# A kernel of linear attention and two feed-forward blocks: its unit loop written as one order, y in its own PSUM banks, a new order for the first units, and the decode steps of the last stage moved

## The chip, the cores and the metric

The kernel runs on one core of one Trainium2 chip. The metric is device time in microseconds, from the start to the end of one execution. Inputs and output lie in the chip's memory (HBM). The reference computes in float32, and the kernel keeps that precision on TensorE by splitting numbers into a high and a low part (below).

## The reference

Attention runs for 4 batches, 8 heads, 768 steps and a head width of 48; its output is a matrix `x` of 3072 tokens by 384. Two feed-forward blocks follow.

```python
for t in range(S):                                  # attention, per batch and head
    cur = einsum('bhd,bhe->bhde', u[None] * k_t, v_t)
    y_t = einsum('bhd,bhde->bhe', r_t, state + cur)
    state = w_t[..., None] * state + einsum('bhd,bhe->bhde', k_t, v_t)

h = x @ w_in                                        # first block, 384 -> 1024
e = exp(h - max(h)); solu = h * e / (sum(e) + 1e-9)
ln = (solu - mean(solu)) / sqrt(var(solu) + 1e-6) * g_ln
x = ln @ w_out                                      # 1024 -> 384

h = x @ w_in2                                       # second block, 384 -> 2048
out = maximum(0.01 * h, h) @ w_out2                 # 2048 -> 384
```

## The kernel before

**Numbers.** The weights of the feed-forward blocks arrive as float64 words. The kernel decodes them itself: one step on VectorE takes the exponent (L112), ScalarE turns it into a float's exponent (L114), and four more VectorE instructions (L120 to L126) make the value. Each float32 operand of a large product is then split into a rounded high part (a ScalarE copy, names in `h`) and the rest (a subtraction, names in `l`), and each product is three products: high by high, high by low, low by high (`passes`).

**Units.** The 3072 tokens are 24 units of 128; unit i is chunk i // 4 of batch i % 4. One unit goes through these steps, each a Python function that issues a few instructions:

- `load_tr`, `load_nat`: loads from SyncE's (SP's) queue. `prep1` to `prep4`, `prep_k`: two scans along time and products with r and k on VectorE (`prep_k` on GpSimd from unit 5 on). `prep_check`: a test of w on ScalarE. `prep_state`, `prep_bonus`, `prep_vd`: GpSimd; `prep_diag`: VectorE.
- `att_scores`: four transposes of k (L441, into the PSUM bank PK) and 32 products of k and r (L445, into PA). `att_evac_s` and `att_evac_k` take them out of PSUM. `att_u`: 32 products that give the state's increments (L465, also PA). `att_mid`, `att_mul_next`, `att_state`: the state, on VectorE (ScalarE for units 0 to 3), GpSimd, VectorE.
- `att_y`: 64 small products that add up y (L499, L509, L518) in PA. `att_x`: two VectorE additions that read y. `x_t`: three transposes into PZ[0] (L530); `x_hi`, `x_lo`: the split of x.
- `mm1`: h in two halves of nine products (L547, into PH). `soft_max` (maximum on VectorE, exponential on ScalarE), `soft_z` (product on VectorE, a factor on GpSimd), `soft_c`, `soft_q` (ScalarE). `z_t`: eight transposes into both PZ banks (L573), `z_hi`, `z_lo`: their split in two halves each.
- `mm2`: after units 4, 5, ... one product of the block's second matrix for a group of three units, in two halves of twelve products (L596, PO or PK); `mm2_out` sends it to HBM.

**Order.** Everything stands in a `manual_schedule`: each engine works off its instructions in the order in which the program names them, and waits for what the others owe it. The functions are called in three ways. The first units (0 to 12, with the parts of others that belong there) follow a list, the text `FIRST` (L31), in which the decode of the first block's weights, `w1_a` to `w1_d`, is mixed with the units. Then a loop (L847 to L906) does units 12 to 22, and a written tail (L916 to L979) the rest. In the loop, the small products of a unit stand in three places: scores, then half an `mm2`, `att_u`, `z_t` and `mm1`, then y, then the other half of `mm2`.

**Last stage.** The second feed-forward block has 96 steps (6 groups of 512 tokens by 16 chunks of the 2048 columns). Step n does `mm3`: nine products into one of two PSUM buffers `h2` (L753), then a scaled copy on ScalarE (L760), a maximum on VectorE that also reads the buffer (L761) and a rounding copy on ScalarE (L762). `gw_sub` is the low part, on VectorE (L767), which reads L762's result. `mm4` for step n - 2 (L777) is nine products that read both parts. The weights of this block are decoded in `dec_step`, one of 32 chunks a time in three phases (so 34 calls): L112 and L114 of a new chunk, L731 (ScalarE) for an older one, L120 to L126 of the one before, and L732 (VectorE). Two calls stand at the end of the loop, five in the tail, and one in each step of the last stage until the chunks are done, except in steps 3, 7 and 11:

```python
g, c = order[n]
mm3(g, c)
if n % 4 != 3 or n > 12:
    dec_step()
gw_sub(g, c)
...
if 2 <= n < len(order) - 1:
    mm4(*order[n - 2])
```

At the start, all four parts of the first block's weights are issued among the first units' loads (`load_w1i`, `load_w1o`, L796 to L803), the first of them from ScalarE's queue.

Of the kernel before, what the change touches and what calls it, by code (L numbers as in the profile page):

```python
# [31 lines left out]
load_nat 2; att_scores 0; w1_a; prep_state 1; w1_a; w1_a; att_evac_s 0; att_evac_k 0; att_u 0; att_mid 0;
prep1 1; w1_c; w1_d; w1_b; w1_b; w1_b; w1_b; att_mul_next 0; prep_check 1; prep_diag 0; prep_k 1; prep_vd 0;
prep_check 2; prep2 1; att_state 0; w1_c; w1_d; w1_c; w1_a; prep3 1; prep4 1; load_tr 3; w1_d; att_y 0;
w1_c; w1_b; w1_d; att_x 0; w1_c; w1_d; load_nat 3; att_scores 1; x_t 0; w1_c; x_hi 0; prep1 2; w1_a; w1_a;
att_evac_s 1; prep2 2; prep_bonus 1; att_evac_k 1; att_u 1; x_lo 0; mm1 0 0; w1_b; w1_d; w1_c; prep3 2;
att_mid 1; w1_a; att_mul_next 1; mm1 0 1; prep_diag 1; w1_b; att_state 1; prep_vd 1; prep_check 3; att_y 1;
w1_a; w1_d; w1_a; w1_b; w1_b; w1_c; w1_d; w1_c; att_x 1; prep_bonus 2; soft_max 0; w1_d; x_t 1; x_hi 1;
prep_k 2; prep4 2; load_tr 4; load_nat 4; att_scores 2; att_evac_k 2; prep_diag 2; prep_vd 2; soft_z 0;
soft_c 0; att_evac_s 2; att_u 2; w1_c; prep1 3; x_lo 1; z_t 0; soft_q 0; prep_k 3; z_hi 0 0; mm1 1 0; prep2  # L40
3; prep3 3; mm1 1 1; att_mid 2; w1_a; z_hi 0 1; w1_a; w1_a; w1_b; att_mul_next 2; w1_d; w1_c; w1_d; z_lo 0
0; w1_b; w1_c; att_state 2; att_y 2; soft_max 1; prep_check 4; w1_b; prep4 3; load_tr 5; w1_b; prep_bonus 3;
w1_d; w1_c; att_x 2; x_t 2; x_hi 2; w1_d; soft_z 1; soft_c 1; x_lo 2; prep_diag 3; prep1 4; load_nat 5;
att_scores 3; prep_vd 3; att_evac_s 3; prep_state 2; mm1 2 0; att_evac_k 3; w1_c; att_u 3; mm1 2 1; att_mid
3; prep2 4; z_lo 0 1; z_t 1; prep_check 5; prep3 4; prep4 4; w1_d; prep_k 4; load_tr 6; att_mul_next 3; z_hi
1 0; att_state 3; att_y 3; prep1 5; soft_q 1; soft_max 2; z_lo 1 0; prep_bonus 4; att_x 3; load_nat 6;
att_scores 4; att_evac_k 4; prep_state 3; soft_z 2; att_evac_s 4; x_t 3; x_hi 3; prep_state 4; x_lo 3; att_u
4; prep_bonus 5; prep_check 6; z_hi 1 1; att_mid 4; att_mul_next 4; prep_diag 4; prep_vd 4; prep2 5; prep3
5; prep_diag 5; mm1 3 0; mm1 3 1; prep_k 5; att_state 4; z_lo 1 1; att_y 4; soft_c 2; soft_q 2; soft_max 3;
prep4 5; load_tr 7; z_t 2; z_hi 2 0; att_x 4; load_nat 7; att_scores 5; z_lo 2 0; x_t 4; prep_bonus 6;  # L50
soft_z 3; att_evac_k 5; x_hi 4; x_lo 4; prep_vd 5; mm2 0 0 0; att_evac_s 5; prep1 6; prep_k 6; mm1 4 0; z_hi
2 1; z_lo 2 1; prep_state 5; att_u 5; att_mid 5; prep2 6; att_mul_next 5; att_state 5; soft_c 3; mm1 4 1;
prep1 7; soft_q 3; z_t 3; soft_max 4; att_y 5; mm2 0 0 1; prep3 6; prep4 6; load_tr 8; att_x 5; load_nat 8;
att_scores 6; z_hi 3 0; prep_diag 6; z_lo 3 0; x_t 5; z_hi 3 1; z_lo 3 1; prep_state 6; prep_vd 6; prep_k 7;
soft_z 4; mm2_out 0 0; mm2 0 1 0; x_hi 5; x_lo 5; mm1 5 0; att_evac_k 6; att_evac_s 6; att_u 6; mm1 5 1;
prep2 7; prep3 7; soft_c 4; soft_q 4; att_mid 6; prep4 7; att_mul_next 6; att_state 6; prep_check 7; load_tr
9; prep_state 7; z_t 4; z_hi 4 0; z_hi 4 1; att_y 6; soft_max 5; z_lo 4 0; prep1 8; mm2 0 1 1; mm2_out 0 1;
att_x 6; load_nat 9; att_scores 7; prep_bonus 7; att_evac_k 7; soft_z 5; x_t 6; x_hi 6; z_lo 4 1; mm2 0 2 0;
soft_c 5; att_evac_s 7; att_u 7; x_lo 6; prep_diag 7; mm1 6 0; prep_vd 7; att_mid 7; att_mul_next 7;
prep_check 8; z_t 5; prep2 8; prep3 8; z_hi 5 0; soft_q 5; z_hi 5 1; prep_k 8; att_state 7; att_y 7; prep4  # L60
8; load_tr 10; att_x 7; z_lo 5 0; mm1 6 1; soft_max 6; prep_bonus 8; prep_bonus 9; load_nat 10; att_scores
8; att_evac_s 8; mm2 0 2 1; z_lo 5 1; prep_state 8; att_evac_k 8; soft_z 6; x_t 7; att_u 8; mm2_out 0 2; mm2
1 0 0; att_mid 8; x_hi 7; x_lo 7; mm1 7 0; prep_check 9; att_mul_next 8; mm1 7 1; soft_c 6; z_t 6; soft_q 6;
prep1 9; prep_diag 8; prep2 9; z_hi 6 0; z_hi 6 1; prep3 9; att_state 8; prep4 9; soft_max 7; z_lo 6 0; z_lo
6 1; prep_state 9; prep_vd 8; att_y 8; prep_k 9; load_tr 11; mm2 1 0 1; mm2_out 1 0; att_x 8; x_t 8; x_hi 8;
load_nat 11; att_scores 9; prep1 10; soft_z 7; prep_diag 9; mm2 1 1 0; att_evac_k 9; prep_bonus 10;
att_evac_s 9; att_u 9; x_lo 8; prep2 10; prep3 10; prep_check 10; mm1 8 0; prep4 10; prep_vd 9; soft_c 7;
z_t 7; att_mid 9; z_hi 7 0; mm1 8 1; prep_diag 10; att_mul_next 9; att_state 9; att_y 9; z_lo 7 0;
prep_check 11; prep1 11; soft_q 7; soft_max 8; mm2 1 1 1; z_hi 7 1; prep_k 10; load_tr 12; prep_k 11;
prep_bonus 11; att_x 9; prep2 11; prep_state 10; soft_z 8; mm2_out 1 1; x_t 9; x_hi 9; load_nat 12;  # L70
att_scores 10; att_evac_k 10; x_lo 9; att_evac_s 10; mm2 1 2 0; att_u 10; soft_c 8; att_mid 10; soft_q 8;
att_mul_next 10; z_lo 7 1; prep_vd 10; mm1 9 0; mm1 9 1; z_t 8; att_state 10; att_y 10; prep3 11; prep4 11;
load_tr 13; mm2 1 2 1; z_hi 8 0; soft_max 9; z_lo 8 0; att_x 10; x_t 10; z_hi 8 1; soft_z 9; x_hi 10; x_lo
10; load_nat 13; att_scores 11; att_evac_s 11; prep_diag 11; mm2_out 1 2; z_lo 8 1; prep_vd 11; soft_c 9;
mm2 2 0 0; prep1 12; prep_state 11; prep2 12; att_evac_k 11; soft_q 9; att_u 11; att_mid 11; prep_state 12;
att_mul_next 11; z_t 9; z_hi 9 0; z_hi 9 1; prep3 12; prep4 12; prep_k 12; att_state 11; prep_check 12;
load_tr 14; mm1 10 0; mm1 10 1; z_lo 9 0; z_lo 9 1; prep_bonus 12; att_y 11; soft_max 10; att_x 11; mm2 2 0
1; mm2_out 2 0; x_t 11; soft_z 10; load_nat 14; att_scores 12; x_hi 11; att_evac_k 12; prep_diag 12; x_lo
11; att_evac_s 12; prep_vd 12; soft_c 10; mm2 2 1 0; prep1 13; prep2 13; soft_q 10; att_u 12; att_mid 12;
prep_state 13; att_mul_next 12; z_t 10; z_hi 10 0; z_hi 10 1; prep3 13; prep4 13; prep_k 13; att_state 12;  # L80
prep_check 13; load_tr 15; mm1 11 0; mm1 11 1; z_lo 10 0; z_lo 10 1; prep_bonus 13; att_y 12; soft_max 11;
# [992 lines left out]
```

## Time and profile before

| | |
|---|---|
| time of three runs, us | 792.67, 792.75, 793.3 (median 792.75) |
| profiled execution, us | 787.38 |
| its span, first to last instruction, us | 785.7 |
| mean granted clock of TensorE | 0.988 of full speed |
| busy: TensorE, VectorE, ScalarE, GpSimd, us | 738.6, 541.0, 354.4, 166.1 |
| share of TensorE on the chain that ended last | 87% |

The profiled execution was 5.4 us below the median of the timed runs. Busy shares are means over stages with different limits; a busy TensorE is a queue of matmuls that overlap, so its pace is read from the distance between the starts of its instructions, not from their lengths. TensorE's clock has two levels, 1.2 and 2.4 GHz; "granted clock" is the mean share of the full one over a stretch.

### The profile page before, as it was taken

Reading aid. Unit: us, or ns where it says so; the run is one execution under the profiler, and the core shown is the slowest. Engines: PE = TensorE matmul, PEld = TensorE weight load, DVE = VectorE, ACT = ScalarE, POOL = GpSimd, SP = SyncE. Lnnn points to the kernel's source line nnn. Section 1 sums busy time; section 2 is a strip of 40 time slices with the busy share of each in tenths; the row PEclk is TensorE's granted clock in tenths of the full one; section 3 lists DMA queues with packets and bytes.
Section 4 is the critical chain, followed back from the end, with each engine's and each line's share of the span. In section 5 each row is a group of like instructions: output and inputs, shape, how many; then the busy total and the mean of one; then the engine's idle time right before and its main releaser. Section 6 shows DMA issues by size and latency. Waiting matters only on the chain.

```text
span 785.7 us, 14941 instructions
## 1 busy us (share of the span) xinstructions
PE 738.6 (94%) x6197; PEld 617.7 (79%) x6197; DVE 541.0 (69%) x866; ACT 354.4 (45%) x648; POOL 166.1 (21%) x181
## 2 busy tenths in 40 slices
PE   2487899999999999999999999999999999999996
...
DVE  5989988888888888877798899853333334334333
...
GB/s 293 258 42 66 102 97 127 111 135 91 133 99 124 145 142 126 86 16 112 145 137 153 77 98 100 15 147 1 0 1 81 0 1 41 0 1 41 0 1 43
DMA packets 31261, 66.60 MB, mean 85 GB/s; under 512 B 4188, under 2 KB 16628, under 8 KB 31060
## 3 DMA queue, kind: packets, MB, share of 16 engines
...
q14 instruction: 23, 0.19, 0.1%
...
## 4 chain that ended last, share of the span: by engine, by line
PE 87%; DVE 6%; DMA 3%; SPq 1%; ACT 1%; issue 1%; POOL 0%; DVEq 0%; ACTq 0%
PE acc L777 25%; PE h L753 24%; PE PO L596 12%; PE PH L547 11%; PE PZ L573 2%; PE PA L509 2%; DMA tr<-in_trw_dram 2%; PE PA L445 2%; PE PA L465 2%; PE PK L596 2%; PE PA L518 1%; PE PZ L530 1%; DMA natq<-in_nat_dram 1%; PE PK L441 1%; DVE e L398 1%; PE PO L663 1%
## 5 line engine op out<-in xcount | busy, mean ns | idle before, releaser
L761 DVE TENSOR_TENSOR t<-t,h 128x512 f32<-128x512 f32 x96 | 66.0, 688 | 124.5 <-ACT t L760 124.3
L760 ACT ACTIVATE t<-h 128x512 f32<-128x512 f32 x96 | 57.5, 598 | 163.8 <-PE h L753 163.8
L777 PE MATMUL acc<-gw,w2oh 128*128 128x512 f32 x288 | 112.3, 390 | 0.5 <-DVE gw L767 0.5
L777 PE MATMUL acc<-gh,w2oh 128*128 128x512 f32 x288 | 112.2, 390 | 0.0
L777 PE MATMUL acc<-gh,w2ol 128*128 128x512 f32 x288 | 112.1, 389 | 0.0
L753 PE MATMUL h<-x2l,w2ih 128*128 128x512 f32 x288 | 112.1, 389 | 0.0
L753 PE MATMUL h<-x2h,w2il 128*128 128x512 f32 x288 | 112.1, 389 | 0.0
L753 PE MATMUL h<-x2h,w2ih 128*128 128x512 f32 x288 | 112.0, 389 | 0.0
L767 DVE TENSOR_TENSOR gw<-t,gh 128x512 fp32r<-128x512 f32 x96 | 69.5, 724 | 47.5 <-ACT gh L762 47.5
L762 ACT CAST gh<-t 128x512 fp32r<-128x512 f32 x96 | 59.7, 622 | 78.2 <-DVE t L761 78.2
L744 POOL TENSOR_TENSOR x2l<-x2l,x2h 128x1536 fp32r<-128x1536 f32 x4 | 14.0, 3508 | 279.7 <-ACT x2h L740 164.6
L777 PEld LDWEIGHTS acc<-gw,w2oh 128*128 128x128 f32 x288 | 54.1, 188 | 12.1 <-DVE gw L767 0.9
L777 PEld LDWEIGHTS acc<-gh,w2ol 128*128 128x128 f32 x288 | 54.0, 188 | 11.8
L753 PEld LDWEIGHTS h<-x2h,w2il 128*128 128x128 f32 x288 | 54.1, 188 | 11.3
L753 PEld LDWEIGHTS h<-x2h,w2ih 128*128 128x128 f32 x288 | 54.1, 188 | 11.3
L753 PEld LDWEIGHTS h<-x2l,w2ih 128*128 128x128 f32 x288 | 54.0, 188 | 11.1
L777 PEld LDWEIGHTS acc<-gh,w2oh 128*128 128x128 f32 x288 | 54.0, 188 | 11.1
L596 PE MATMUL PO<-zh,w1oh 128*128 128x384 f32 x168 | 60.4, 359 | 0.0
L547 PE MATMUL PH<-w1ih,xh 128*128 128x512 f32 x144 | 59.3, 412 | 0.6 <-ACT xh L535 0.6
L547 PE MATMUL PH<-w1il,xh 128*128 128x512 f32 x144 | 56.8, 395 | 0.0
L547 PE MATMUL PH<-w1ih,xl 128*128 128x512 f32 x144 | 56.8, 394 | 0.0
L596 PE MATMUL PO<-zh,w1ol 128*128 128x384 f32 x168 | 56.5, 336 | 0.0
(154 smaller groups left out, 1453.3 us busy)
## 6 DMA issues: line engine op xcount, KB each, us to landing
...
w2s<-in_moe_w_in_dram SPq DMA_DIRECT2D x48, 128.0 KB, 2.3
...
```

The costliest lines, as they stand in the source:

```text
L445: pe.matmul(out=PA[64 * c:64 * c + 64, x, 64 * a:64 * a + 64], lhsT=kt[p:q, 2 * a + c], rhs=lt[p:q, 2 * a + c], start=True, stop=True)
L465: pe.matmul(out=PA[64 * x:64 * x + m, c, 256 + 48 * q:304 + 48 * q], lhsT=ks[64 * c:64 * c + 64, 112 * q + 64 * x:112 * q + 64 * x + m], r ...
L509: pe.matmul(out=y[64 * c:64 * c + 64, hs], lhsT=s[64 * c:64 * c + 64, x, q], rhs=a[64 * c:64 * c + 64, h], start=(h == 0), stop=False, ski ...
L547: pe.matmul(out=PH[:, half], lhsT=a[:, kc], rhs=c[:, kc, 512 * half:512 * half + 512], start=(n == 0), stop=(n == 8))
L573: pe.transpose(PZ[c // 4][:, 128 * (c % 4):128 * (c % 4) + 128], zbuf[:, 128 * c:128 * c + 128], ident)
L596: pe.matmul(out=o2[m], lhsT=a[:, c, 128 * m:128 * m + 128], rhs=d[:, c], start=(c == 0 and q == 0), stop=(c == K1 - 1 and q == 2))
L753: pe.matmul(out=h2, lhsT=a[:, kc, 128 * o:128 * o + 128], rhs=d[:, kc], start=(q == 0), stop=(q == 8))
L760: act.activation(out=t, in_=h2, func=AF.Copy, scale=0.01)
L761: dve.tensor_tensor(out=t, in0=t, in1=h2, op=ALU.max)
L762: act.copy(out=gh, in_=t)
L767: dve.tensor_tensor(out=gw, in0=t, in1=f(gh), op=ALU.subtract)
L777: pe.matmul(out=at, lhsT=a[:, c % 4, 128 * o:128 * o + 128], rhs=d, start=(c == 0 and q == 0), stop=(c == K2 - 1 and q == 2))
```

## The change

The loop is now a text as well, `LOOP`, whose numbers are added to the unit i. It starts at unit 10, and a unit's small products stand in one row: y of unit i, scores and u of unit i + 1. The transposes of k are a function of their own, `att_kt`. y is added up in the two PZ banks instead of PA. `FIRST` is a new list for units 0 to 9; the loads of the first weights are in it, behind the first five loads of `tr` and `nat`. In the tail, the order is changed and there are six decode steps instead of two and five. In the last stage the decode step stands ahead of `mm3`, in every step.

```diff
-FIRST_UNITS = 12
+FIRST_UNITS = 10
 FIRST = """
...
+prep1 0; load_u; prep_check 0; load_nat 0; prep2 0; prep_state 0; prep3 0; load_tr 1; prep_k 0; load_nat 1; prep4 0;
+att_scores 0; att_evac_s 0; att_kt 0; att_evac_k 0; att_u 0; prep_bonus 0; load_g; prep_diag 0; att_mid 0;
+att_mul_next 0; att_state 0; prep_vd 0; prep1 1; prep2 1; load_tr 2; prep_k 1; att_y 0; w1_g; prep3 1; att_x 0;
+prep_bonus 1; load_i 0; att_kt 1; prep4 1; prep_state 1; x_t 0; att_evac_k 1; x_hi 0; x_lo 0; att_u 1; att_scores 1;
+prep1 2; att_mid 1; prep_diag 1; prep2 2; att_evac_s 1; att_mul_next 1; att_state 1; w1_a; prep_state 2; prep_k 2;
+prep3 2; load_i 1; prep_check 1; w1_b; w1_a; att_kt 2; prep4 2; w1_a; w1_c; w1_d; w1_b; w1_c; w1_a; w1_b; w1_d;
+w1_c; w1_a; load_o 0; w1_d; mm1 0 0; w1_a; prep_vd 1; w1_b; w1_c; load_tr 3; prep_check 2; w1_d; load_tr 4; w1_b;
+att_y 1; load_nat 2; prep_bonus 2; w1_c; w1_b; w1_d; w1_a; w1_a; w1_c; w1_a; w1_a; w1_d; w1_b; w1_b; mm1 0 1; prep1
...
+8 1; att_evac_k 10; prep1 11; prep_state 10; z_hi 7 1; prep_k 11; prep2 11; mm2b 8; att_evac_s 9; z_lo 7 0; z_lo 7
+1; att_state 9; att_scores 10; soft_max 8; att_y 9; load_nat 11; mm2_out 8; att_x 9; att_u 10; soft_e 8; att_kt 11;
...
+LOOP = """
+att_y 0; soft_max -1; soft_e -1; load_nat 3; att_scores 1; att_u 1; att_x 0; att_evac_s 1; soft_z -1; soft_nm -1;
+att_mid 1; mm2a 0; x_t 0; att_mul_next 1; x_hi 0; soft_c -1; prep3 2; x_lo 0; mm2b 0; mm2_out 0; prep_state 2;
+prep4 2; load_tr 4; att_state 1; z_t -1; att_kt 2; prep_diag 2; prep_vd 2; z_hi -1 0; z_hi -1 1; att_evac_k 2;
+z_lo -1 0; z_lo -1 1; soft_q -1; prep_bonus 3; prep_check 3; mm1 0 0; mm1 0 1; prep1 3; prep2 3; prep_k 3
 """
...
-        def att_scores(i):
-            lt, kt = L[i], kh.pop(i)
+        def att_kt(i):
+            kt = kh[i]
             for a in range(4):
                 pe.transpose(PK[:, 112 * a:112 * a + 112], flat(kt[0:112, 2 * a:2 * a + 2]), ident[0:112, 0:112])
+
+        def att_scores(i):
+            lt, kt = L[i], kh[i]
...
         def att_y(i):
...
-            y0, y1 = PA[:, 0, 0:384], PA[:, 1, 0:384]
+            y0, y1 = PZ[0][:, 0:384], PZ[1][:, 0:384]
...
-            dve.tensor_tensor(out=flat(x), in0=PA[:, 0, 0:384], in1=flat(vds.pop(i)), op=ALU.add)
-            dve.tensor_tensor(out=flat(x), in0=PA[:, 1, 0:384], in1=flat(x), op=ALU.add)
+            dve.tensor_tensor(out=flat(x), in0=PZ[0][:, 0:384], in1=flat(vds[i]), op=ALU.add)
+            dve.tensor_tensor(out=flat(x), in0=PZ[1][:, 0:384], in1=flat(x), op=ALU.add)
...
+            run(FIRST)
             for i in range(FIRST_UNITS, NU - 1):
...
                 if 15 <= i < 19:
                     load_w2()
...
+                run(LOOP, i)
+
+            i = NU - 1
+            att_y(i)
+            soft_max(i - 1)
+            soft_e(i - 1)
+            att_x(i)
+            soft_z(i - 1)
+            soft_nm(i - 1)
+            mm2(6, 1, 0)
+            dec_step()
+            x_t(i)
+            x_hi(i)
+            x_lo(i)
...
             soft_c(i - 1)
+            mm2(6, 1, 1)
+            mm2_out(6, 1)
+            z_t(i - 1)
+            z_hi(i - 1, 0)
+            z_hi(i - 1, 1)
+            z_lo(i - 1, 0)
+            z_lo(i - 1, 1)
             soft_q(i - 1)
             dec_step()
             mm1(i, 0)
             mm1(i, 1)
             soft_max(i)
-            z_t(i - 1)
+            soft_e(i)
             soft_z(i)
-            z_hi(i - 1, 0)
-            z_hi(i - 1, 1)
-            mm2(6, 1, 0)
-            mm2(6, 1, 1)
+            soft_nm(i)
+            mm2(6, 2, 0)
             soft_c(i)
-            z_lo(i - 1, 0)
-            z_lo(i - 1, 1)
-            mm2_out(6, 1)
             dec_step()
-            mm2(6, 2, 0)
+            mm2(6, 2, 1)
             z_t(i)
             z_hi(i, 0)
             z_hi(i, 1)
-            mm2(6, 2, 1)
             z_lo(i, 0)
             z_lo(i, 1)
...
                 g, c = order[n]
+                dec_step()
                 mm3(g, c)
-                if n % 4 != 3 or n > 12:
-                    dec_step()
                 gw_sub(g, c)
```

`run` calls the functions that the text names. `mm2a`, `mm2b` and `mm2_out` of unit i are the two halves and the output of the `mm2` that belongs to it; `soft_e` and `soft_nm` are the second instructions of the old `soft_max` and `soft_z`; `load_i` and `load_o` are the old loads of the weights by halves, `w1_g` and `load_g` those of `g_ln`.

## Rows read from the trace of the kernel before

**Rows 1.** Page, part 2: busy tenths of two engines in 40 slices of 19.64 us.
```profile
PE   2487899999999999999999999999999999999996
...
DVE  5989988888888888877798899853333334334333
```

**Rows 2.** Windows: stretch, length, busy us (instructions) of PE, PEld, DVE, ACT, POOL; clock, DMA.
```profile
60.00:80.00 20.00, 15.67 (x156) 11.87 (x156) 19.62 (x33) 11.93 (x24) 3.93 (x5) 0.74 0.24 65
...
0.00:109.86 109.86, 70.62 (x808) 50.14 (x808) 93.88 (x154) 55.73 (x112) 34.68 (x48) 0.92 0.48 150
...
109.86:350.00 240.14, 239.70 (x3408) 210.54 (x3408) 203.27 (x290) 131.60 (x253) 112.18 (x126) 1.00 0.37 111
```

**Rows 3.** Timeline of TensorE in one loop unit: start, us, engine, line, operation, tiles, count.
```profile
239.57 0.35 PE L441 MATMUL PK<-ident,kt 112*128 112x112 f32 x2
...
239.67 0.26 PE L441 MATMUL PK<-ident,kt 112*128 112x112 f32 x1
239.86 0.69 PE L445 MATMUL PA<-lt,kt 48*64 48x64 f32 x32
...
240.33 0.22 PE L445 MATMUL PA<-lt,kt 48*64 48x64 f32 x1
240.48 0.44 PE L596 MATMUL PO<-zh,w1oh 128*128 128x384 f32 x1
240.76 0.34 PE L596 MATMUL PO<-zl,w1oh 128*128 128x384 f32 x1
...
242.50 0.34 PE L596 MATMUL PO<-zh,w1ol 128*128 128x384 f32 x1
242.77 0.67 PE L465 MATMUL PA<-natv,ks 64*64 64x48 f32 x32
...
243.21 0.22 PE L465 MATMUL PA<-natv,ks 64*64 64x48 f32 x2
243.37 1.09 PE L573 MATMUL PZ<-ident,zbuf 128*128 128x128 f32 x8
```

**Rows 4.** Timeline of TensorE: first products of units 4, 10, 22 and last stage.
```profile
109.86 0.39 PE L547 MATMUL PH<-w1ih,xh 128*128 128x512 f32 x1
...
191.39 0.48 PE L547 MATMUL PH<-w1ih,xh 128*128 128x512 f32 x1
...
349.87 0.48 PE L547 MATMUL PH<-w1ih,xh 128*128 128x512 f32 x1
...
386.30 0.39 PE L753 MATMUL h<-x2h,w2ih 128*128 128x512 f32 x1
```

**Rows 5.** Timeline of VectorE in steps 3 and 4 of the last stage.
```profile
401.19 0.68 DVE L761 TENSOR_TENSOR t<-t,h 128x512 f32<-128x512 f32 x1
402.56 0.69 DVE L767 TENSOR_TENSOR gw<-t,gh 128x512 fp32r<-128x512 f32 x1 [0.69 <-ACT gh L762]
403.17 0.68 DVE L761 TENSOR_TENSOR t<-t,h 128x512 f32<-128x512 f32 x1
403.77 0.35 DVE L112 TENSOR_SCALAR w2t<-w2s 128x384 int32<-128x384 int32 x1
...
406.56 0.69 DVE L767 TENSOR_TENSOR gw<-t,gh 128x512 fp32r<-128x512 f32 x1
```

**Rows 6.** Chain that ended last: start, us, nine products of one `mm3`, step 28.
```profile
497.86 2.04 PE h L753 x9
```

**Rows 7.** Timeline of VectorE at the start: first scans of units 0 and 1.
```profile
4.36 1.24 DVE L380 TENSOR_TENSOR_SCAN suf<-tr,sel 112x520 f32<-112x520 f32 x1 [2.17 <-DMA tr<-in_trw_dram]
...
19.70 1.24 DVE L380 TENSOR_TENSOR_SCAN suf<-tr,sel 112x520 f32<-112x520 f32 x1 [3.08 <-DMA tr<-in_trw_dram]
```

**Rows 8.** Timeline of the tail: TensorE's z_t of unit 22, ScalarE's soft_c, VectorE's z_lo.
```profile
363.37 1.03 PE L573 MATMUL PZ<-ident,zbuf 128*128 128x128 f32 x8
...
367.67 1.16 ACT L563 ACTIVATE zbuf<-zbuf,nm_all 128x1024 f32<-128x1024 f32 x1 [0.61 <-POOL nm_all L559]
...
371.77 1.29 DVE L586 TENSOR_TENSOR zl<-PZ,zh 128x512 fp32r<-128x512 f32 x2 [0.42 <-ACT zh L582]
```

More of the change, by code (lines that the diff above doesn't have):

```diff
@@ L29 @@
 TRW = 1545
-FIRST_UNITS = 12
+FIRST_UNITS = 10
 FIRST = """
[L32 to L81, printed above, removed]
@@ new lines @@
+0; soft_nm 0; prep_check 3; load_o 1; w1_d; att_evac_s 2; soft_c 0; soft_q 0; x_lo 1; prep2 3; att_mul_next 2; prep3
+3; mm1 1 0; w1_c; w1_d; w1_c; w1_b; w1_a; w1_a; w1_d; prep_k 3; z_t 0; prep4 3; w1_b; load_nat 3; z_hi 0 0; att_kt
+3; prep1 4; mm1 1 1; att_evac_k 3; z_lo 0 0; z_hi 0 1; prep_diag 2; prep_vd 2; w1_c; z_lo 0 1; att_state 2; att_y 2;
+soft_max 1; load_tr 5; att_u 3; att_x 2; att_scores 3; w1_d; prep_bonus 3; soft_e 1; x_t 2; w1_c; load_nat 4; prep_k
+4; att_mid 3; soft_z 1; x_hi 2; prep_check 4; prep_bonus 4; x_lo 2; att_kt 4; att_mul_next 3; soft_nm 1; mm1 2 0;
@@ new lines @@
+w1_d; soft_c 1; att_evac_s 3; prep2 4; prep3 4; w1_a; w1_b; prep4 4; mm1 2 1; z_t 1; soft_q 1; z_hi 1 0; w1_b;
+att_evac_k 4; prep_diag 3; att_state 3; prep_state 3; z_lo 1 0; w1_c; z_hi 1 1; z_lo 1 1; prep_vd 3; att_scores 4;
+prep_state 4; prep_check 5; att_u 4; att_y 3; soft_max 2; prep1 5; w1_d; prep_state 5; att_x 3; w1_c; soft_e 2;
+soft_z 2; prep_k 5; x_t 3; att_kt 5; soft_nm 2; x_hi 3; x_lo 3; mm1 3 0; prep2 5; soft_c 2; w1_d; prep3 5; w1_a; z_t
+2; att_evac_s 4; mm1 3 1; prep_diag 4; w1_b; z_hi 2 0; att_mid 4; load_nat 5; z_lo 2 0; att_evac_k 5; z_hi 2 1;
@@ new lines @@
+prep4 5; att_mul_next 4; z_lo 2 1; w1_c; load_tr 6; att_scores 5; prep_check 6; load_tr 7; w1_d; att_state 4;
+prep_bonus 5; load_nat 6; soft_max 3; prep1 6; att_y 4; prep2 6; prep_vd 4; att_x 4; prep_diag 5; att_u 5; mm2a 4;
+soft_q 2; soft_e 3; att_evac_s 5; soft_z 3; prep_state 6; prep_k 6; att_mid 5; x_t 4; x_hi 4; x_lo 4; soft_nm 3;
+mm2b 4; prep_bonus 6; prep3 6; att_mul_next 5; att_state 5; mm1 4 0; prep_vd 5; mm2_out 4; soft_c 3; att_kt 6; prep4
+6; z_t 3; soft_q 3; mm1 4 1; z_hi 3 0; load_nat 7; load_tr 8; z_hi 3 1; z_lo 3 0; att_scores 6; z_lo 3 1; att_evac_k
```

172 lines of the change are left out of this document (60 added, 112 removed).

## The prediction, made before the change was timed

> **What bounds the kernel now.** I read the forty slices first, then windows, then single instructions. The slices [rows 1] show two regimes. Over the first five slices (98 us) VectorE is at 8 to 9 tenths and TensorE below it; from there TensorE is at 9 to the end. The windows put numbers to it [rows 2]: up to 109.86 us VectorE is busy 93.88 us, so it idles 16.0, while TensorE has worked 70.6. So the start is worth what VectorE's queue saves; after it only what stands in TensorE's own queue counts, until something makes that queue wait.
>
> Three milestones of TensorE frame the sum [rows 4]: the first product `mm1` of unit 4 starts at 109.86, of unit 10 at 191.39, of unit 22 at 349.87; the first product of the last stage, `mm3`, at 386.30. Units 4 to 10 take 81.53 / 6 = 13.59 us each, units 10 to 22 (158.48 / 12) 13.21. The last stage issues nine products of `mm3` and nine of `mm4` a step, 2.04 us each [rows 6], 4.08 a step.
>
> **Term 1, small matmuls in one block.** The timeline of a unit shows what a change between small (64-wide) and full matmuls costs [rows 3]. Into the scores: 0.19 us after the last `kt` transpose, whose own pitch is 0.10 (239.57 to 239.67): 0.09 lost. Out of them: 0.15 to the first `mm2` product and then 0.28 to the second, where small groups start about 0.04 apart and `mm2` has a pitch of (242.50 - 240.76) / 10 = 0.17: 0.11 + 0.11. Into `att_u`: 242.50 to 242.77, 0.27 for 0.17: 0.10. Out of it into `z_t`: 0.15, so 0.11, and some 0.06 in `z_t`'s first step. Sum 0.58. A unit has three such blocks (y, scores, u); with y, scores and u in a row two entries and two exits go, which are just these; I take 0.6. Above it is 0.7 (the slower first groups of both blocks); below it 0.3, if a change from one small kind to the next costs half an entry-and-exit, which no row here shows. I stay near the upper end, since each gap above has a full matmul on one side. No instruction is added on TensorE: `att_kt` is the four transposes that stood in `att_scores`.
>
> A loop unit so falls from 13.21 to 12.6, if nobody else makes TensorE wait. Over the 240.14 us from unit 4 to unit 22 VectorE is busy 203.27, ScalarE 131.60 and GpSimd 112.18 [rows 2], so 11.3, 7.3 and 6.2 a unit; they have room. y in the two PZ banks lifts the wait of the next scores for `att_x`, but puts y behind `z_lo`. That one ends some 2 us before y in the loop. The first units' order is also written with the three parts together, but before, the written units ran 0.38 above the loop's pace (13.59 against 13.21); I take 12.85 for the six units 4 to 10 (bounds 12.6 and 13.3). 6 x 12.85 + 12 x 12.6 = 228.3 us in place of 240.0. The other edits issue the same instructions: reads in place of pops, `soft_e` and `soft_nm` under names of their own, `load_i` from SP's queue instead of ScalarE's.
>
> **Term 2, the start.** VectorE lost time there to loads: it waits 2.17 us for the first `tr` and 3.08 for the second [rows 7], because all of w1 (6.3 MB in `load_w1i`, `load_w1o`) is issued among them. In the new order five loads of `tr` and `nat` go ahead of `load_i 0`; the first `tr` then should come about 1 us earlier and the second before it is wanted. In exchange, three units' attention now runs ahead of the decode, one instruction after the other: scores, `ks`, u, GpSimd's product and y of unit 0 leave VectorE about 5 us idle. SP's queue has a new risk, `load_tr 4` waiting for `prep_check 2` with `load_nat 2` and `load_o 1` behind it; what they bring is wanted some 15 us later. With the initial wait (3.3) and about 2 more of waits for the exponent step on ScalarE and for y, I count 10 us idle in place of 16 (bounds 6 and 16). VectorE does 2.8 us more ahead of the product `mm1 4 0` (`att_mid 5`, `att_state 5`, `prep2 6`, `prep3 6`, `z_lo 2 1`): 93.9 + 2.8 + 10 = 106.7, I take 106.5. TensorE has by then also done u of unit 5 and both halves of the first `mm2` instead of one (2.2 us, taken off the tail below). `mm1` of unit 22 then starts at 106.5 + 228.3 = 334.8, against 349.87.
>
> **Term 3, from unit 22 to the last stage.** Before: 386.30 - 349.87 = 36.4. Off goes the half `mm2` just named, 2.2. Two waits come. From the end of `mm1 23` to the end of `soft_c` ScalarE and VectorE need 5.5 us (363.37 to 367.67 + 1.16 [rows 8]); before, `z_t 22` and three halves of `mm2` lay beside it, now two halves (4.4): 1.1 us. After `z_t 23` VectorE must end both `z_lo` (1.29 [rows 8]) behind a decode step before the next `mm2` can start; before, a half `mm2` covered that, now nothing does: about 2.2. A third of 0.3 stands ahead of `z_t 22`; about 0.8 of old waits go. 36.4 - 2.2 + 3.6 - 0.8 = 37.0, so the last stage starts at 371.8, 14.5 us earlier than before.
>
> **Term 4, the decode step ahead of `mm3`.** This one loses. VectorE's queue in a step was: max (L761), decode (L112 to L732), subtraction (L767). The subtraction needs ScalarE's copy of what the max wrote, and the decode lay in that gap. Where a step had no decode the gap shows [rows 5]: L761 at 401.19, L767 at 402.56 with 0.69 idle before it. With the decode the step takes 0.60 (403.17 to 403.77) + 2.79 (to 406.56) + 0.61 (402.56 to 403.17) = 4.00, just under TensorE's 4.08. In the new order the decode comes first, then max, wait, subtraction: 2.79 + 1.37 + 0.61 = 4.77 a step, and the steps 3, 7 and 11 that had no decode get one. VectorE becomes the bound at 0.69 us a step. `mm3` of step n needs the bank that the max of step n - 2 frees. Six decode steps stand ahead of the stage and 34 are needed, so steps 0 to 27 carry one, 26 of them whole. The decode of step 0 puts its max 3.6 us behind the first product (in place of 2.9), so its bank is free at 4.3; step 28 starts 4.3 + 26 x 4.77 - 0.3 = 128.0 us after the stage's start. Before it started 497.86 - 386.30 = 111.6 after it [rows 4, 6]. Loss 16.4 (bounds 14.5 and 18). The two steps of slack between `mm3` and `mm4` are already in that count; after step 28 TensorE is the bound again and nothing is given back.
>
> **Sum.** -14.5 + 16.4 = +1.9 us on the profiled execution's 787.38 (span 785.7 and 1.7 around it), 789.3. That execution was 5.4 below the median of the runs, 792.75, so the forecast is 792.75 + 1.9 = 794.6.
>
> **Rivals.** *A, as summed:* 794.6, by itself 791 to 798; chance 0.45. *B, faster:* the decode's loss stays, but VectorE idles only 6 us at the start (-4) and the new first units run at the loop's 12.6 (-1.5): 789.1. For it speaks that almost all of the 6 us of load waits above can go; against it, that written units were slower than the loop before. It decides from 3.5 us less at the start on. Chance 0.23. *C, slower by a wait in the loop:* `soft_c` now stands on ScalarE behind `x_hi`, and that behind `x_t`; counted from y's first product, y, scores and u end at 2.55, half an `mm2` at 4.75, `x_t` and `x_hi` let `soft_c` (1.16 [rows 8]) start at 5.7 and end at 6.9, and `z_t`'s turn comes at 7.16. If `att_x` is late behind `soft_max` and the margin of 0.26 is overrun by 0.4, each of 18 units pays it: 7.2 us, 801.8. Before, other `mm2` products lay there. Chance 0.22. *D, the new decode place does nothing:* if the two steps' slack swallowed the wait, the gain alone stays: 778.3. Against it, 26 x 0.69 is 18 us and the slack under 5. Chance 0.05. *E, the clock:* TensorE's clock was granted at 0.74 of full speed between 60 and 80 us, where TensorE worked 15.67 of 20 us with pauses, so part of that stretch was at 1.2 GHz [rows 2]. If the long block of small matmuls brought such a fall once a unit, with 1.4 us lost in it, 18 units cost 25: 820. From 109.86 us on it was granted in full, with the small blocks apart [rows 2]. Chance 0.05. [...]
>
> **How the numbers follow.** A change under 0.2% (1.6 us) can't be told from none here. Faster: B almost whole (0.20), D (0.05) and a low part of A (0.08): 0.33. Same: the middle of A (0.16) and edges of B and C: 0.20. Slower: the rest of A (0.21), C, E: 0.47. The range 786 to 803 holds A, most of B and of C; the bounds of the terms (4 us either way at the start, 3 in the units, 2 in the last stage) fill it.
>
> **What would show it.** Right: `mm1` of successive loop units 12.6 apart; `mm3` steps 4.77 apart up to step 28 and 4.08 after; VectorE idle 0.7 before L767 in each of these; the first `mm1` of unit 4 near 106. Wrong: steps of 4.1 all through the last stage (term 4), units at 13 with TensorE waiting for `soft_c` or `z_lo` (term 1), a start past 110 or under 103 (term 2), the granted clock under 1 after 110 us.

## The result and the profile after

The changed kernel takes 795.39 us (median of 20 runs, 793.91 to 797.6), the kernel before 789.47 in the same session (20 runs, 785.91 to 793.38); ratio 1.0069, 95% interval [1.005, 1.0088]: slower by 4 to 7 us. Forecast were 794.6 and +1.9 us. The absolute time came out closer than the difference by luck: before's 20 runs here fall in two groups, eleven from 785.91 to 789.61 and nine from 792.34 to 793.38, and the three runs shown above all lay in the upper one, so that its median was 3.3 us lower here. The profiled executions differ by 6.7 us (794.06 against 787.38; spans 792.4 and 785.7), and it is these that the terms below explain.

Page, part 2 of the kernel after, 40 slices of 19.81 us; it answers to [rows 1]:

```profile
PE   3668799999999999998989999999999999999997
...
DVE  5989997868887888657888888653334334334333
...
PEclk9989999999999999999999999999999999999999
```

TensorE is at 9 tenths from the sixth slice on, as before, but for 8 in the 19th and the 21st (tail and last stage), and VectorE stands at 6 to 8 through the loop. The page shows no stage in which TensorE is plainly short of work; for that the stretch has to be cut finer. Windows of the kernel after, cut at the same milestones of TensorE as in the prediction (columns as in [rows 2]: stretch, length, busy us of PE, PEld, DVE, ACT, POOL, granted clock, DMA share, GB/s):

```profile
0.00:105.31 105.31, 71.26 (x851) 50.82 (x852) 91.92 (x157) 55.47 (x111) 27.66 (x48) 0.97 0.52 155
105.31:187.82 82.51, 78.47 (x1135) 69.88 (x1135) 66.89 (x101) 46.02 (x88) 43.28 (x47) 1.00 0.41 117
187.82:338.17 150.35, 150.35 (x2244) 136.93 (x2242) 121.01 (x183) 85.16 (x165) 76.52 (x80) 1.00 0.40 114
338.17:376.71 38.54, 35.46 (x246) 32.69 (x245) 26.38 (x48) 20.72 (x35) 0.47 (x2) 0.96 0.35 108
376.71:505.49 128.78, 118.15 (x489) 90.56 (x488) 107.96 (x221) 57.23 (x109) 4.20 (x1) 0.99 0.30 94
505.49:792.40 286.91, 281.85 (x1242) 233.10 (x1242) 110.19 (x158) 90.80 (x144) 14.02 (x4) 1.00 0.08 26
```

The difference of length and busy time is TensorE's idle time: none in the twelve loop units (third row), 4.04 us in units 4 to 10, 3.08 in the tail, 10.6 in the first 28 steps of the last stage. Against [rows 4]: unit 4 starts 4.55 us earlier (105.31 for 109.86), unit 22 11.70 earlier (338.17 for 349.87), the last stage 9.59 earlier (376.71 for 386.30). The 497.86 of [rows 6] is from the chain; the timeline of the kernel before has the first product of step 28 at 497.70:

```profile
497.70 0.39 PE L753 MATMUL h<-x2h,w2ih 128*128 128x512 f32 x1
```

So step 28 starts 7.8 later (505.49). 9.6 us were won ahead of the last stage, 17.4 lost in its first 28 steps, and 1.1 won behind them (286.91 for 288.00).

One loop unit on TensorE (timeline; it answers to [rows 3]):

```profile
238.08 0.48 PE L548 MATMUL PH<-w1ih,xh 128*128 128x512 f32 x1
...
242.36 0.27 PE L500 MATMUL PZ<-zero 48*64 48x192 bf16 x2
...
243.72 0.24 PE L447 MATMUL PA<-lt,kt 48*64 48x64 f32 x2
...
244.27 0.62 PE L467 MATMUL PA<-natv,ks 64*48 64x48 f32 x30
244.82 0.45 PE L601 MATMUL PO<-zh,w1oh 128*128 128x384 f32 x1
245.11 0.34 PE L601 MATMUL PO<-zl,w1oh 128*128 128x384 f32 x1
...
250.64 0.48 PE L548 MATMUL PH<-w1ih,xh 128*128 128x512 f32 x1
```

y, scores and u run as one block of 2.46 us (242.36 to 244.82), the second `mm2` product comes 0.29 us after the first (0.28 in [rows 3]), and the next unit's first product is 12.56 us after this one's. One step of VectorE in the last stage (timeline; it answers to [rows 5]; the max is L771 in the changed kernel, ScalarE's copy L772, the subtraction L777):

```profile
395.33 0.68 DVE L771 TENSOR_TENSOR t<-t,h 128x512 f32<-128x512 f32 x1
396.70 0.69 DVE L777 TENSOR_TENSOR gw<-t,gh 128x512 fp32r<-128x512 f32 x1 [0.69 <-ACT gh L772]
397.31 0.36 DVE L111 TENSOR_SCALAR w2t<-w2s 128x384 int32<-128x384 int32 x1
...
400.10 0.68 DVE L771 TENSOR_TENSOR t<-t,h 128x512 f32<-128x512 f32 x1
```

Max, 0.69 us of waiting for ScalarE's copy, subtraction, decode, and the next max 4.77 us after the last. VectorE keeps this pace through the first 25 steps. TensorE's own steps do not: those of `mm3` are 4.77 in steps 2 to 7, 9.54 at step 8, 4.25 at step 9, 4.08 in steps 10 to 15, and 4.77 again in steps 17 to 26. At step 8 the transpose of the scales (`scales`, L796) takes one of the two banks of `mm3` (timeline of TensorE; first products of `mm3` of steps 8 and 9 around it):

```profile
410.38 0.50 PE L763 MATMUL h<-x2h,w2ih 128*128 128x512 f32 x1 [0.39 <-DVE t L771]
...
415.24 0.37 PE L796 MATMUL h<-ident,csc 128*24 128x128 f32 x1 [2.52 <-DVE t L771]
...
419.92 0.50 PE L763 MATMUL h<-x2h,w2ih 128*128 128x512 f32 x1 [0.84 <-DVE t L771]
```

TensorE falls a step back there and makes it up at 4.08 a step, while VectorE goes on at 4.77; so step 28 still comes when VectorE's pace lets it.

### The profile page after: what moved, and what is told of

It is laid out like the page before. It is cut to its first block, busy times and chain, and to the rows that moved or that the text cites. A ratio compares the mean times of both kernels' runs of the same rounds, so it can differ in the third digit from the quotient of the medians.

```text
span 792.4 us, 14979 instructions
## 1 busy us (share of the span) xinstructions
PE 735.5 (93%) x6197; PEld 614.0 (77%) x6197; DVE 524.3 (66%) x866; ACT 355.4 (45%) x648; POOL 166.2 (21%) x181
## 4 chain that ended last, share of the span: by engine, by line
PE 65%; DVE 22%; ACT 4%; DMA 4%; issue 3%; POOL 1%; SPq 0%; DVEq 0%; ACTq 0%; POOLq 0%
PE acc L787 19%; PE h L763 18%; PE PH L548 9%; PE PO L601 9%; DMA tr<-in_trw_dram 2%; DVE t L771 2%; PE PZ L510 2%; PE PZ L578 2%; ACT gh L772 2%; DVE w2s L123 2%; DVE w2t L119 2%; DVE gw L777 1%; DVE w2s L121 1%; PE PA L447 1%; PE PZ L519 1%
## 5 line engine op out<-in xcount | busy, mean ns | idle before, releaser
L771 DVE TENSOR_TENSOR t<-t,h 128x512 f32<-128x512 f32 x96 | 65.8, 686 | 122.1 <-ACT t L770 122.1
L763 PE MATMUL h<-x2h,w2ih 128*128 128x512 f32 x288 | 114.5, 397 | 8.1 <-DVE t L771 8.0
L777 DVE TENSOR_TENSOR gw<-t,gh 128x512 fp32r<-128x512 f32 x96 | 69.4, 723 | 66.2 <-ACT gh L772 66.2
L772 ACT CAST gh<-t 128x512 fp32r<-128x512 f32 x96 | 59.9, 624 | 95.3 <-DVE t L771 95.3
L763 PEld LDWEIGHTS h<-x2l,w2ih 128*128 128x128 f32 x288 | 54.1, 188 | 10.6
## 6 DMA issues: line engine op xcount, KB each, us to landing
w2s<-in_moe_w_in_dram SPq DMA_DIRECT2D x48, 128.0 KB, 2.3
```

The costliest lines, as they stand in the source:

```text
L763: pe.matmul(out=h2, lhsT=a[:, kc, 128 * o:128 * o + 128], rhs=d[:, kc], start=(q == 0), stop=(q == 8))
L771: dve.tensor_tensor(out=t, in0=t, in1=h2, op=ALU.max)
L772: act.copy(out=gh, in_=t)
L777: dve.tensor_tensor(out=gw, in0=t, in1=f(gh), op=ALU.subtract)
```

## The experiments

All run on one core; each ratio is to the kernel before, timed on the same chip. Milestones (first products on TensorE) come from each kernel's profile, which is one execution.

**The decode back between `mm3` and the subtraction**, in the changed kernel:

```
-                dec_step()
                 mm3(g, c)
+                dec_step()
                 gw_sub(g, c)
```

> The changed kernel with one edit: the last stage's decode step goes back between mm3 and the subtraction L777, in every step. Theory (VectorE's queue): the step's bound falls from 2.79 + 1.37 + 0.61 = 4.77 us to TensorE's 4.08, so step 28 starts 112 to 114 us behind the stage's first product in place of 128.8, the time falls by 15 to 17 us and the ratio to the kernel before is 0.985 to 0.988. Rival (slack): the two steps between mm3 and mm4 swallow the wait and the 4.77 steps have another cause, a decode in each step without a pause: steps stay above 4.5 and the ratio stays at 1.005 to 1.009.

Measured: 777.98 us, ratio 0.9838 [0.98, 0.9876]. From step 3 on the steps are 4.08 except two (6.20 and 4.21, steps 8 and 9), and step 28 starts 113.25 us behind the first product. The span is 18.6 us shorter than the changed kernel's: 15.5 in these steps, 1.6 in the tail (the clock, below), 1.1 at the start. The rival falls: with a decode in each step and no pause the steps are 4.08. VectorE's subtraction no longer waits (timeline):

```profile
408.65 0.68 DVE L771 TENSOR_TENSOR t<-t,h 128x512 f32<-128x512 f32 x1
409.25 0.35 DVE L111 TENSOR_SCALAR w2t<-w2s 128x384 int32<-128x384 int32 x1
...
412.04 0.69 DVE L777 TENSOR_TENSOR gw<-t,gh 128x512 fp32r<-128x512 f32 x1
412.64 0.68 DVE L771 TENSOR_TENSOR t<-t,h 128x512 f32<-128x512 f32 x1
```

The 6.20 us stand at step 8, where `scales` takes a bank; VectorE, at 4.00 of 4.08 us a step (408.65 to 412.64), had not yet made up what it was late at the start of the stage.

**The same move alone in the kernel before** (its `if n % 4 != 3 or n > 12` goes as well):

> The kernel before with one edit: its decode step of the last stage goes ahead of mm3, in every step. Theory (VectorE's queue): steps of 4.77 us up to about step 27, the stage loses 15 to 18 us and nothing else moves, ratio 1.019 to 1.023. Rival (the loss belongs to the changed kernel's shorter run-up, six decode steps ahead of the stage in place of seven): under 8 us, ratio up to 1.010.

Measured: 804.46 us, ratio 1.0184 [1.0142, 1.0225]. VectorE's maxima are 4.77 apart, and step 28 comes 128.35 us behind the first product in place of 111.4; the span is 802.6, 16.9 more. The ratio is just under the forecast range, the loss inside its 15 to 18 us. The loss is the move's and owes nothing to the rest of the change.

**The decode stays first, the subtraction is issued a step later:**

```
                 dec_step()
                 mm3(g, c)
-                gw_sub(g, c)
+                if n:
+                    gw_sub(*order[n - 1])
...
+            gw_sub(*order[-1])
```

> The changed kernel, decode still ahead of mm3, but the subtraction L777 of a step is issued one step later, behind the next step's decode and max, so that ScalarE's copy is long done. Theory (the wait max, copy, subtraction is the loss): VectorE has 2.79 + 0.60 + 0.61 = 4.00 us a step, the steps are 4.08, ratio 0.985 to 0.989 as with the decode back in its place. Rival (the max itself comes too late behind the decode and holds the bank of mm3): steps stay above 4.4 and the ratio above 1.000.

Measured: 779.76 us, ratio 0.9858 [0.9822, 0.9895]; steps of 4.08 but for steps 2, 8 and 9 (5.65, 5.00, 4.23), step 28 at 112.84. This is the run that settles the mechanism. VectorE's queue in it (timeline):

```profile
426.85 0.69 DVE L771 TENSOR_TENSOR t<-t,h 128x512 f32<-128x512 f32 x1
427.45 0.69 DVE L777 TENSOR_TENSOR gw<-t,gh 128x512 fp32r<-128x512 f32 x1
428.05 0.35 DVE L111 TENSOR_SCALAR w2t<-w2s 128x384 int32<-128x384 int32 x1
...
430.93 0.69 DVE L771 TENSOR_TENSOR t<-t,h 128x512 f32<-128x512 f32 x1
```

The max still stands behind the decode, yet nothing waits: the subtraction now is the one of the step before, whose copy is long made. It was the wait of the subtraction that cost, not a late max.

**u apart from y and scores**, in the loop's order (part of `LOOP`, its lines joined):

```
-load_nat 3; att_scores 1; att_u 1; att_x 0; att_evac_s 1; soft_z -1; soft_nm -1; att_mid 1; mm2a 0; x_t 0;
+load_nat 3; att_scores 1; att_x 0; att_evac_s 1; soft_z -1; soft_nm -1; mm2a 0; att_u 1; att_mid 1; x_t 0;
```

> The changed kernel with u of the next unit taken out of the block of small matmuls in the loop and put behind the first half of mm2. Theory (each change between small and full matmuls costs some 0.1 to 0.2 us): one more entry and exit a unit, 0.25 to 0.35 us, so a loop unit takes 12.8 to 12.9 us in place of 12.56 and the time grows by 3 to 4.5 us, ratio 1.010 to 1.013. Rival (the loop's gain came from waits that went, not from the changes of shape): 12.5 to 12.6 a unit and a ratio of 1.005 to 1.009.

Measured: 798.71 us, ratio 1.0096 [1.0058, 1.0134]; 12.89 us a unit, in every unit but the last (12.49 for 12.16). The ratio lies between the two ranges, so the pace of the units decides, and it is the theory's. One block more costs 0.33 us; the two that the change took away, 13.21 - 12.56 = 0.65.

**y in the banks of scores and u again, in the loop**, so that `att_x` must stand ahead of the scores:

```
+            if i >= FIRST_UNITS:
+                return PA[:, 0, 0:384], PA[:, 1, 0:384]
...
-load_nat 3; att_scores 1; att_u 1; att_x 0; att_evac_s 1;
+load_nat 3; att_x 0; att_scores 1; att_u 1; att_evac_s 1;
```

> The changed kernel, but in the loop units (10 to 23) y is written to the banks of the scores and u, as in the kernel before, and so att_x stands ahead of the scores. Theory (one block needs y in banks of its own): the scores then wait for both additions of att_x, which end 1.5 to 1.6 us after y's last product (243.72 to 245.24 us in the unit at 238), and TensorE has nothing between; a loop unit goes from 12.56 to 14.0 to 14.2 us, the 13 units lose 18 to 21 us, ratio 1.029 to 1.035. Rival (the banks do not matter, att_x is hidden): 12.6 a unit and 1.005 to 1.009. Rival (the pauses also bring the granted clock down): over 15 a unit, ratio above 1.045.

Measured: 815.14 us, ratio 1.0304 [1.0246, 1.0361]; 14.06 us a unit. The waits of TensorE (line waited for: us in total, times, longest):

```profile
PE PA L447 <- DVE x L531: 17.9, 13, 2.1
```

Thirteen units, each with scores that wait for `att_x` (L531 there). The one block pays only with banks of its own for y.

**Two moves in the first units' order**: `prep1 1; prep2 1` ahead of `prep_diag 0`, and (part of `FIRST`, its lines joined)

```
-z_hi 8 0; prep1 12; prep_vd 11; prep_state 11; mm1 9 1; prep_check 12; prep_k 12; prep3 11; soft_q 8; prep_bonus 12; att_state 10; z_lo 8 0; z_hi 8 1; prep4 11; z_lo 8 1; mm2b 9;
+z_hi 8 0; prep_vd 11; prep_state 11; mm1 9 1; z_hi 8 1; att_state 10; z_lo 8 0; z_lo 8 1; prep1 12; prep_check 12; prep_k 12; prep3 11; soft_q 8; prep_bonus 12; prep4 11; mm2b 9;
```

> The changed kernel with two moves in the order written for the first units: prep1 1 and prep2 1 ahead of prep_diag 0, which waited 3.84 us for GpSimd's first product at 13.53; and z_lo 8 ahead of prep1 12 and prep3 11, since y 10 waited 0.96 us for z_lo at 179.54. Theory (VectorE's queue sets the start; z_lo holds back y in the written units): the idle time before prep_diag 0 falls by the 1.4 to 2.2 us of work put into it, the first product of unit 4 starts at 103 to 104 in place of 105.3, and units 9 to 10 take 15.9 to 16.2 us in place of 17.0; together 2 to 3 us, ratio 1.002 to 1.006. Rival (the start hangs on the loads and on the chain from scores to y of the first units, not on VectorE's sum): unit 4 at 105 to 105.6, ratio 1.005 to 1.009.

Measured: 795.2 us, ratio 1.0057 [1.0026, 1.0088], which the ranges of both share, so the milestones decide. Unit 9 to 10 took 15.74 us in place of 17.04: the wait for `z_lo` was real. Unit 4 started at 104.79, within what the old order gave (104.2 to 108.1, below): the rival holds at the start. The timeline of VectorE there, first of the kernel after, then of this one, shows why:

```profile
13.53 0.55 DVE L427 TENSOR_REDUCE dg<-natq 128x8 f32<-128x384 f32 x1 [3.84 <-POOL natq L423]
...
14.84 1.46 DVE L379 TENSOR_TENSOR_SCAN suf<-tr,sel 112x520 f32<-112x520 f32 x1
```

```profile
13.98 1.24 DVE L379 TENSOR_TENSOR_SCAN suf<-tr,sel 112x520 f32<-112x520 f32 x1 [4.29 <-DMA tr<-in_trw_dram]
...
15.37 0.52 DVE L427 TENSOR_REDUCE dg<-natq 128x8 f32<-128x384 f32 x1
```

The scan of unit 1, put first, waits as long for its own load (4.29 us) as the reduction waited for GpSimd's product of `nat` 0.

**w1's loads as early as before**: `load_i 0` ahead of `load_nat 0`, `load_i 1` ahead of `load_tr 1`.

> The changed kernel, but the loads of w1's first half are issued as early as in the kernel before: load_i 0 ahead of the loads of nat 0, load_i 1 ahead of tr 1. Theory (in the start VectorE waits for loads, and their order is what the new order gained): VectorE's idle time up to unit 4 goes from 13.4 to 17 to 21 us, the first product of unit 4 starts 4 to 8 us later than 105.3, ratio 1.012 to 1.017. Rival (what the start gained comes from the order of the engines' work): under 1.5 us later, ratio 1.005 to 1.009.

Measured: 802.71 us, ratio 1.0144 [1.0086, 1.0201]; unit 4 at 115.04, 9.7 us later, with 23.6 us idle on VectorE (115.04 - 91.45 busy), both above the forecast ranges. The scan of unit 1 waits longest:

```profile
22.97 1.24 DVE L379 TENSOR_TENSOR_SCAN suf<-tr,sel 112x520 f32<-112x520 f32 x1 [6.41 <-DMA tr<-in_trw_dram]
```

So the place of these loads is worth more than the whole 4.55 us that the start gained: with them in front, the new start is slower than the old one (115.04 against 109.86). The old load order itself was not run with the new start; it issued the first of these loads from ScalarE's queue.

**Flag's product behind half an `mm2`, scales at step 28**, on top of the decode back:

```
-            pe.matmul(out=PA[0:1, 0, 0:1], lhsT=anyf, rhs=ones, start=True, stop=True)
...
             mm2(7, 0, 0)
+            pe.matmul(out=PA[0:1, 0, 0:1], lhsT=anyf, rhs=ones, start=True, stop=True)
...
-                if n == 8:
+                if n == 28:
```

> The kernel with the decode back (e1_decode_back) and two more edits, each read from its own stretch. The flag's product on TensorE, which waits for VectorE's flag reduction behind z_lo 23, goes behind the half mm2 that it held up; and the transpose of the scales goes from step 8 of the last stage to step 28, when no decode is left. Theory: from mm1 of unit 22 to the last stage 36.1 to 36.4 us (in e1_decode_back 36.9, in the changed kernel 38.5 with the granted clock under 1 behind the two pauses), and step 8 takes 4.1 to 4.3 us in place of 6.20, together 2.3 to 2.9 us below e1_decode_back, ratio 0.979 to 0.982. Rival for the scales (VectorE gives back the lost 2.1 us anyway, as its queue is 4.00 against 4.08): step 28 starts where it did and the ratio stays at 0.984. Rival for the tail: the pauses still bring the clock down, 37.8 to 38.5 us.

Measured: 775.45 us, ratio 0.9797 [0.9743, 0.9852]; tail 36.27 us, step 8 4.08, step 28 at 111.41 in place of 113.25. That is what the theory had in both stretches.

**The best of these together**, with the second move of the first units' order:

> The version that the runs point to: the kernel with the flag's product and the scales moved (e7_tail_and_scales) and the second move of e6_first_order alone, z_lo 8 ahead of prep1 12 and prep3 11. If each stretch keeps what it gave by itself: units 9 to 10 in 15.7 to 16.0 us in place of 17.0, the tail at 36.3, step 28 of the last stage 111.4 behind its first product; 1.2 us below e7_tail_and_scales, ratio 0.976 to 0.981. Rival (VectorE gives the 1.3 us back in the next units, as its queue is only moved): ratio 0.980 to 0.984 and the same start of the last stage relative to unit 4.

Measured: 775.97 us, ratio 0.9824 [0.9783, 0.9865]. Units 9 to 10 15.75 us, step 28 at 110.99; but the tail took 37.80 in this profile, with the clock at 0.66 (360 to 365 us) behind the pauses, which ate the 1.3 us. The ratio is in the rival's range, though VectorE did not give the 1.3 us back: the tail lost as much.

**The load of tr 1 ahead of nat 0**, and `prep1`, `prep2`, `prep_k`, `prep3` of unit 1 ahead of `prep_diag 0`, on top of that:

> e9_best with another order at the very start: the load of tr 1 ahead of the load of nat 0, and prep1, prep2, prep_k and prep3 of unit 1 ahead of prep_diag 0, so that VectorE has 3.4 us of work while nat 0 comes. Theory (the start hangs on which load comes when VectorE wants it; in e6_first_order the wait only went from nat 0 to tr 1): tr 1 lands by 9 to 10 us, VectorE's waits for loads up to unit 4 fall from 5.5 to 2 to 3.5 us and the first product of unit 4 starts 2 to 3 us earlier, at 102 to 104; ratio 0.973 to 0.978. Rival (the chain from nat 0 over u and y of unit 0 to x 0 sets the start): unit 4 at 104.5 to 108, as nat 0 comes 2 us later, ratio 0.977 to 0.982.

Measured: 775.06 us, ratio 0.9806 [0.9765, 0.9847]. VectorE's waits for loads fell to 1.9 us in all, but unit 4 started at 105.20: the time came back as waits for products and copies of units 0 and 1 (`w2s` for ScalarE 2.6, `xl` 1.7, `x` 1.6). Ratio and start are the rival's. Profiles with one and the same start order put unit 4 anywhere from 104.2 to 108.1, so a gain under 2 us there stays open.

**The pauses of before with the new run-up**: in the kernel with the decode back, no decode in steps 3, 7 and 11.

> The kernel with the decode back (e1_decode_back) and also without a decode in steps 3, 7 and 11, as in the kernel before: the last stage as it was before, and all else as changed. Theory (a decode in each step leaves VectorE at 4.00 of 4.08 us a step and late by nearly one step, so that the scales' transpose at step 8 makes TensorE wait 1.55 us; the pauses give VectorE 2.79 us each): step 8 takes 4.1 to 4.3 us in place of 6.20, step 28 comes 111.3 to 111.8 us behind the stage's first product in place of 113.3, ratio 0.979 to 0.983. Rival (the pauses are worth nothing; VectorE's lag comes from the inverse deviations in steps 0 to 2): 113 us and 0.983 to 0.986.

Measured: 828.43 us, ratio 1.0486 [1.0444, 1.0529]. Both theories missed: step 8 did take 4.23, but from step 12 on every second step took 9.53. Timeline of TensorE there:

```profile
430.38 0.50 PE L787 MATMUL acc<-gh,w2oh 128*128 128x512 f32 x1 [2.98 <-ACT w2oh L741]
...
431.61 0.79 PE L787 MATMUL acc<-gh,w2ol 128*128 128x512 f32 x1 [0.49 <-DVE w2ol L742]
...
433.05 0.63 PE L787 MATMUL acc<-gh,w2ol 128*128 128x512 f32 x1
433.48 0.63 PE L787 MATMUL acc<-gh,w2oh 128*128 128x512 f32 x1
```

`mm4` waits for weights decoded in this very step, behind the max of the `mm3` just issued, and after 3 us of pause its products stand 0.43 us apart in place of 0.23. The clock was granted at 0.63 from 430.40 to 435.00. The kernel before made seven decode steps ahead of the stage, the changed one six: by this count, with three pauses, that one is missing. So the decode in every step, which cost 1.8 us around the scales, is what the shorter run-up needs.

**TensorE's pauses in the tail filled** with nine products into a bank that is not read, seven ahead of `z_t 23` and two behind it, on top of tr 1 ahead of nat 0:

> e10_tr_ahead_of_nat with nine extra products (128x384, into a bank that nobody reads) in TensorE's queue, seven where it pauses 1.20 us ahead of z_t 23 and two where it waits 0.30 us ahead of the next mm2, so that it hardly pauses there. They add nothing to the result. In three profiles of ten the granted clock stayed at 1.00 behind these pauses and in seven it fell to 0.66 to 0.89 for some 5 to 10 us, which costs 1.5 to 1.6 us. Theory (the pauses are what lets the clock fall): clock 1.00 through the tail and 36.2 to 36.6 us from unit 22 to the last stage in place of 37.8, ratio 0.976 to 0.982. Rival (the fall has another cause, or what counts lies ahead of the pauses): clock under 0.9 and 37.7 to 38.1 us, ratio 0.979 to 0.985. A hold of the clock alone is weak evidence, since three of ten held without the filling; a fall would be strong.

Measured: 772.03 us, ratio 0.978 [0.9749, 0.9812], the fastest version found; tail 36.28 us. The windows of the tail: the kernel after, behind its pauses of 1.20 and 1.73 us; then this one.

```profile
358.00:362.00 4.00, 1.45 (x11) 0.89 (x9) 3.77 (x8) 3.64 (x6) 0.24 (x1) 1.00 0.15 26
362.00:366.00 4.00, 3.62 (x16) 3.58 (x17) 3.41 (x10) 3.10 (x6) 0.00 (x0) 0.74 0.65 186
366.00:370.00 4.00, 4.00 (x21) 4.00 (x21) 3.63 (x6) 0.48 (x1) 0.00 (x0) 0.84 0.66 235
```

```profile
360.00:365.00 5.00, 5.00 (x30) 4.72 (x30) 4.42 (x9) 2.89 (x5) 0.00 (x0) 1.00 0.59 179
365.00:370.00 5.00, 5.00 (x31) 5.00 (x30) 3.28 (x6) 2.77 (x4) 0.00 (x0) 1.00 0.65 233
```

That the filling holds the clock agrees with one run; since three profiles of eleven held it without (the expectation above counts ten), that is not shown.

## Why the prediction was right, and where not

**Term 4, the decode ahead of `mm3`: right, in mechanism and size.** VectorE takes 4.77 us a step, step 28 comes at 128.8 (128.0 forecast), 17.4 us are lost (16.4 forecast, with 111.6 for 111.4 as the base). Moved alone it costs 16.9, undone it gives 15.5 back, and with the subtraction a step later the steps are back at 4.08. The sign that the prediction named, steps of `mm3` 4.77 apart up to step 28, came on VectorE; on TensorE the scales' bank broke it at step 8, which the prediction did not see and the sum did not need. Rival D (the slack swallows it) is refuted.

**Term 1 in the loop: right.** 12.56 us (12.6 forecast), and 0.33 a block. Rival C's wait for `soft_c` did not come: TensorE was busy 150.35 of 150.35 us. Rival E's fall of the clock did not come in the loop either: 1.00 with the one block, 2.46 of 12.56 us, in each unit. The Trainium skill, "TensorE: Matmul & The Clock Gate", section "Why this matters for your kernels", has the clock swing for thin matmuls whose loop does not go through all slices of the contraction (K-tiles) before the next DMA; no product of this loop waited for a DMA, so nothing here tests that.

**Term 1 in units 4 to 10: the step that failed.** "I take 12.85 for the six units" made 77.1 us; it took 82.51, 5.4 more. Of these, 4.0 are waiting (78.47 busy), which was left out. The other 1.4 are work: TensorE makes 56 `z_t` and 28 `kt` transposes in this stretch, where six loop units have 48 and 24. Before, the written units had more work than the loop too (one `z_t` and one u), so most of their 0.38 us above its pace was work, and not slowness, as the prediction took it. The prediction saw that y now stands behind `z_lo`, and took the loop's margin of 2 us for the written units too, where there was none. Waits of TensorE in that stretch (columns as above):

```profile
PE PZ L500 <- DVE zl L591: 2.2, 3, 1.0
PE PZ L531 <- DVE x L526: 1.6, 3, 0.8
```

The longest for `z_lo` is 1.01 us, inside the written units:

```profile
125.81 0.24 PE L500 MATMUL PZ<-zero 48*64 48x192 bf16 x1 [1.01 <-DVE zl L591]
```

The two others, 1.2 us together, stand at the seam between written units and loop; they alone were tested by a run (15.74 us for 17.04, above). VectorE, then TensorE at the seam (timelines):

```profile
174.81 2.63 DVE L397 TENSOR_TENSOR_SCAN e<-tr,e 112x520 f32<-112x520 f32 x1
...
178.81 0.68 DVE L591 TENSOR_TENSOR zl<-PZ,zh 128x512 fp32r<-128x512 f32 x1
```

```profile
178.34 0.24 PE L500 MATMUL PZ<-zero 48*64 48x192 bf16 x1 [0.23 <-DVE zl L591]
...
179.54 0.24 PE L500 MATMUL PZ<-zero 48*64 48x192 bf16 x1 [0.96 <-DVE zl L591]
```

**Term 2, the start: right in sum, wrong inside.** Unit 4 at 105.31 (106.5 forecast; 104.2 to 108.1 over the profiles with this start). VectorE idled 13.4 us, not 10: the waits for `tr` fell from 5.3 us [rows 7] to 1.9, about as forecast, but 3.84 us came back in front of `prep_diag 0`, a load wait at one remove. In turn its work was 91.9 us, not 96.7. Rival B (6 us idle) is refuted, and two reorderings did not reach it.

**Term 3, the tail: 38.5 us, forecast 37.0.** The pauses were smaller than forecast (3.08 for 3.6); the clock that fell behind them (0.96 over the tail, 1.00 in the kernel before) was not in the sum. A granted clock under 1 after 110 us was one of the signs that the prediction named for being wrong. The same instructions took 36.91 us in the kernel with the decode back, where the clock held: 1.6 us.

**The sum.** Against the forecast: start -1.2, units 4 to 10 +5.4, loop -0.8, tail +1.5, last stage +1.0, after step 28 -1.1 (286.91 for 288.00): +4.8, and 1.9 + 4.8 is the 6.7 us measured. By its time, 795.39, case A held; by the difference it did not quite, since 792.75 + 6.7 = 799.5 lies above A's 798. That the time lies within 0.8 us of the forecast is luck with before's median.
